# Weights that stay loaded on TensorE in a decode-attention kernel: one q slice for two score matmuls, 24 probability columns for four V matmuls, then a masked sum

## The chip, the cores and the metric

The kernel runs on one core of one Trainium2 chip. The metric is device time in microseconds (us), the median of several executions.

Engine names in the profile: PE is TensorE's matmuls, PEld its weight loads, DVE VectorE, ACT ScalarE, POOL GpSimd, SPq the queue from which the large transfers are issued.

## The reference, cut to what matters

```python
# B=2, Sq=1, Hq=16, Hkv=8, Sk=32768, Dh=256; all bf16
q = (x @ wq) as (B, Hq, 1, Dh);  k, v = caches (B, Hkv, Sk, Dh), each used by 2 q heads
scores = einsum("bhqd,bhkd->bhqk", q, k) * Dh**-0.5
o      = einsum("bhqk,bhkd->bhqd", softmax(scores), v)
a      = o.reshape(B, 1, Hq*Dh) @ wo
out    = g * a + (1 - g) * mlp(x)          # a small MLP, done while the first K arrive
```

The work is reading the two caches: 2 x 2 x 8 x 32768 x 256 bf16 values are 537 MB, and each is used for two heads only.

## The kernel before

There are 16 groups (batch x KV head). A group is two K tiles and two V tiles of 8.39 MB each. A ring of three slots in SBUF takes the tiles in the order K0 K1 K2 V0 K3 V1 K4 V2 ..., so that V runs two tiles behind K. A transfer into a slot is issued when TensorE has finished with the tile that was there.

```python
order: for i: K(i), then V(i - 2)         # slot = position in the order, modulo 3
released = {"K": S of that tile done, "V": PV of that tile done}
SP:  for d in order: wait(PE released the slot's last tile);  dma_start(slot, tile d)
```

DVE transposes each K tile in place in 8 blocks; after each block TensorE multiplies it with 8 slices of the query (each padded into a window, so that successive blocks fill different rows of one PSUM bank):

```python
def S(idx):                                # PE, K tile idx of group g, half t
    for blk in range(8):
        wait(DVE, T(idx, blk))
        for s in range(8):                 # 128x128 weights, 128x512 moving
            matmul(ps_s[g % 2], a_win(g, s, t * 8 + blk), kv[block blk, slice s],
                   start=first, stop=last)

def PV(v):                                 # PE, V tile; four column groups j at a time
    for kk in range(0, 8, 2):
        for r16 in range(16):
            matmul(ps_o[g % 2][32*j : 32*j + 4, 512], PT[:, r16, 4 columns], rows(kk, r16), ...)

def softmax(g):                            # DVE, after the second K tile's S
    MX  = reduce_max(ps_s[g % 2])          # 128x512
    ... maximum over partitions by two tiny matmuls (M1, M2); ACT: pexp = exp(ps_s - max)
    PT[g % 2] = transpose(pexp)            # 128x512
    ls2, L (matmul), rl = 1 / sum

def do_end(g):                             # DVE, after the group's second PV
    o_sb = copy(ps_o[g % 2])               # 128x512, one instruction
    ... OT: 4 tiny matmuls fold the column groups; attnT = OT * rl
# ... cut: projections, MLP, output product, the last group's V, helpers
```

## Time and profile before

| | before |
|---|---|
| time, median (range) | 1282.51 us (1282.38 to 1282.76) |
| PE busy / weight loads busy / DVE busy | 742.5 / 306.7 / 621.8 us |
| HBM read | 547.43 MB |
| instructions | 10758 |

No engine is busy for even 60% of the span, while the DMA engines are at 90% or more in every slice but the last. The line of queue 8 reads: 39 packets, 0.64 MB, 0.2% of the DMA engines' time; these are instructions being fetched for the engines.

Busy times in chosen stretches of before (us of each engine, with the number of instructions, then the granted TensorE clock, the DMA share and the rate):

```profile
core 0: us, PE busy (x) PEld busy (x) DVE busy (x) ACT busy (x) POOL busy (x), PEclk, DMA share, GB/s
104.00:136.00 32.00, 18.52 (x119) 7.18 (x112) 17.66 (x8) 0.00 (x0) 0.00 (x0) 0.79 1.00 433
...
117.80:1207.57 1089.77, 625.90 (x3780) 247.67 (x3780) 537.96 (x350) 22.29 (x94) 0.00 (x0) 0.77 1.00 433
```

In the 1090 us of the steady state the DMA share is 1.00. The rate, 433 GB/s, is that of the ceiling that the Trainium skill gives in "DMA: Bandwidth & Descriptors", section "Where 436 GB/s comes from" (435 GB/s).

The groups of the page of before that the change touches: line, engine, operation, output and inputs, shapes and count, then busy us and mean ns of one, then the idle time before them and what ended it.

```profile
L385 PE MATMUL ps_s<-ring,Abd 128*128 128x512 bf16 x2048 | 529.7, 415 | 435.4 <-DVE ring L604 434.8
L604 DVE STREAM_TRANSPOSE ring<-ring 128x2048 uint32<-128x2048 uint32 x256 | 565.2, 2276 | 418.3 <-DMA ring<-in_A_k_cache_dram 418.3
L385 PEld LDWEIGHTS ps_s<-ring,Abd 128*128 128x128 bf16 x2048 | 200.9, 103 | 758.2 <-DVE ring L604 347.3
...
L439 PEld LDWEIGHTS ps_o<-ring,PT 128*4 128x4 bf16 x1920 | 49.0, 97 | 82.0 <-issue 41.4
L638 DVE COPY o_sb<-ps_o 128x512 f32<-128x512 f32 x15 | 10.4, 692 | 80.7 <-PE ps_o L439 80.7
```

Read the waits from left to right: score matmuls wait 435 us for DVE's transposes, and these wait 418 us for K to arrive. Everything waits for DMA.

One group boundary in before, from the timeline (start us, duration us, what; SPq lines are transfers being issued):

```profile
409.88 0.33 SPq L311 DMA_DIRECT2D ring<-in_A_v_cache_dram  x1
413.45 0.33 SPq L311 DMA_DIRECT2D ring<-in_A_k_cache_dram  x1
428.93 17.66 DVE L604 STREAM_TRANSPOSE ring<-ring 128x2048 uint32<-128x2048 uint32 x8 [21.04 <-DMA ring<-in_A_k_cache_dram]
448.59 0.33 SPq L311 DMA_DIRECT2D ring<-in_A_v_cache_dram  x1
458.27 0.33 SPq L311 DMA_DIRECT2D ring<-in_A_k_cache_dram  x1
468.14 2.31 DVE L604 STREAM_TRANSPOSE ring<-ring 128x2048 uint32<-128x2048 uint32 x1 [7.75 <-DMA ring<-in_A_k_cache_dram]
```

K lands at 428.93; its scores are done 19.66 us later, which frees the slot for the V issued at 448.59. At that moment the K issued at 413.45 is still in flight; it lands at 468.14. So the DMA queue has 19.5 us of work when the slot is freed.

### The profile page before, as it was taken

What the parts mean: (1) busy time and instruction counts of PE and PEld (TensorE: products, weight loads), DVE (VectorE), ACT (ScalarE), POOL (GpSimd) and SP (SyncE); (2) the same over time, 40 slices, a digit from 0 to 9 for tenths busy, and PEclk for the clock granted to TensorE, in tenths of its full rate; (3) what the DMA queues carried; (4) which work ended last, traced back from release to release, by engine and by line L of the source; (5) the groups of instructions that cost most, each with busy time, mean ns of one, the idle gap of its engine ahead of it and who ended that gap; (6) DMA issues with size and microseconds to landing.
All of it is one profiled execution on the core that took longest, in us unless ns stands there. A gap on an engine that the chain in (4) does not pass through costs nothing.

```text
span 1281.1 us, 10758 instructions
## 1 busy us (share of the span) xinstructions
PE 742.5 (58%) x4977; PEld 306.7 (24%) x4977; DVE 621.8 (49%) x421; ACT 29.0 (2%) x118; POOL 3.5 (0%) x12
## 2 busy tenths in 40 slices
PE   4675557645476554665645666454765546656466
PEld 3222222212132121222212222121322212222134
DVE  1784446544365543456534465443655434565330
ACT  1000000000000000000000000000000000000000
POOL 1000000000000000000000000000000000000000
PEclk9887887776887777887777877777886778877786
DMA  9999999999999999999999999999999999999997
GB/s 409 428 435 436 432 432 430 435 432 438 426 433 438 434 424 432 443 429 430 432 440 428 426 438 438 430 424 438 434 432 432 432 432 434 435 432 428 436 401 293
DMA packets 12780, 548.12 MB, mean 428 GB/s; under 512 B 1336, under 2 KB 3520, under 8 KB 3904
## 3 DMA queue, kind: packets, MB, share of 16 engines
q1 hardware_dynamic: 12580, 547.43, 99.1%
q8 instruction: 39, 0.64, 0.2%
q10 hardware_dynamic: 156, 0.01, 0.0%
q14 instruction: 5, 0.04, 0.0%
HBM read 547.43 MB, written 0.00 MB: 427 GB/s over the span
## 4 chain that ended last, share of the span: by engine, by line
DMA 60%; DVE 26%; PE 11%; ACT 1%; SPq 1%; issue 0%; another core or an unknown queue 0%; ACTq 0%
DMA ring<-in_A_k_cache_dram 58%; DVE ring L604 23%; PE ps_o L439 7%; PE ps_s L385 2%; DMA ring<-in_A_v_cache_dram 2%; ACT pexp L536 1%; DVE PT L623 1%; DVE mx L609 1%; SPq L306 1%; PE ps_m L406 1%; PE ps_m L396 0%; PE ps_m L401 0%; DVE gmax L611 0%; DVE gmx L617 0%; ACT negm L532 0%
## 5 line engine op out<-in xcount | busy, mean ns | idle before, releaser
L385 PE MATMUL ps_s<-ring,Abd 128*128 128x512 bf16 x2048 | 529.7, 415 | 435.4 <-DVE ring L604 434.8
L604 DVE STREAM_TRANSPOSE ring<-ring 128x2048 uint32<-128x2048 uint32 x256 | 565.2, 2276 | 418.3 <-DMA ring<-in_A_k_cache_dram 418.3
L385 PEld LDWEIGHTS ps_s<-ring,Abd 128*128 128x128 bf16 x2048 | 200.9, 103 | 758.2 <-DVE ring L604 347.3
L439 PE MATMUL ps_o<-ring,PT 128*4 128x512 bf16 x1920 | 138.4, 453 | 1.0 <-DMA ring<-in_A_v_cache_dram 1.0
L439 PEld LDWEIGHTS ps_o<-ring,PT 128*4 128x4 bf16 x1920 | 49.0, 97 | 82.0 <-issue 41.4
L638 DVE COPY o_sb<-ps_o 128x512 f32<-128x512 f32 x15 | 10.4, 692 | 80.7 <-PE ps_o L439 80.7
L532 ACT ACTIVATE negm<-ps_m 128x1 f32<-128x1 f32 x16 | 2.7, 171 | 1175.4 <-PE ps_m L401 1175.4
L609 DVE TENSOR_REDUCE mx<-ps_s 128x1 f32<-128x512 f32 x16 | 11.1, 692 | 32.2 <-PE ps_s L385 32.2
L406 PE MATMUL ps_m<-ls,ones_f 128*128 128x2 f32 x32 | 7.8, 314 | 30.9 <-DVE ls L624 30.9
L415 PE MATMUL ps_m<-sel,o_sb 128*128 128x2 f32 x120 | 16.6, 260 | 12.0 <-DVE o_sb L638 12.0
L458 PE MATMUL ps_o<-PT,ring 128*128 128x2 bf16 x512 | 14.6, 165 | 14.5 <-DMA ring<-in_A_v_cache_dram 12.6
L623 DVE STREAM_TRANSPOSE PT<-pexp 128x512 bf16<-128x512 bf16 x16 | 11.4, 711 | 23.7 <-ACT pexp L536 23.7
L415 PEld LDWEIGHTS ps_m<-sel,o_sb 128*128 128x128 f32 x120 | 15.3, 196 | 19.6 <-DVE o_sb L638 19.6
L643 DVE TENSOR_TENSOR attnT<-ps_o,rl 128x2 bf16<-128x2 f32 x2 | 0.2, 158 | 37.6 <-PE ps_o L458 37.6
L458 PEld LDWEIGHTS ps_o<-PT,ring 128*128 128x128 bf16 x512 | 14.0, 103 | 15.5 <-DMA ring<-in_A_v_cache_dram 13.5
L406 PEld LDWEIGHTS ps_m<-ls,ones_f 128*128 128x128 f32 x32 | 6.5, 252 | 32.2 <-DVE ls L624 32.2
L396 PE MATMUL ps_m<-ident_f,mx 128*1 128x128 f32 x32 | 6.1, 270 | 12.5 <-DVE mx L609 12.5
L527 ACT COPY Abd<-qrep 32x16 bf16<-32x16 bf16 x64 | 12.7, 199 | 0.6
L643 DVE TENSOR_TENSOR attnT<-ps_m,rl 128x2 bf16<-128x2 f32 x30 | 3.4, 157 | 17.9 <-PE ps_m L415 17.9
L401 PE MATMUL ps_m<-ones_f,gmx 1*128 1x1 f32 x32 | 6.0, 256 | 9.9 <-DVE gmx L617 9.9
L536 ACT ACTIVATE pexp<-ps_s,negm 128x512 bf16<-128x512 f32 x16 | 11.0, 687 | 0.5
L468 PE MATMUL ps_f<-ring,attnT 128*2 128x448 bf16 x32 | 10.0, 488 | 0.7 <-DMA ring<-in_A_wo_dram 0.4
(58 smaller groups left out, 69.3 us busy)
## 6 DMA issues: line engine op xcount, KB each, us to landing
ring<-in_A_v_cache_dram SPq DMA_DIRECT2D x1, 4096.0 KB, 28.9
ring<-in_A_wo_dram SPq DMA_DIRECT2D x1, 3584.0 KB, 19.1
ring<-in_A_wq_dram SPq DMA_DIRECT2D x1, 3072.0 KB, 10.4
ring<-in_A_v_cache_dram SPq DMA_DIRECT2D x1, 2048.0 KB, 23.6
ring<-in_B_w_dram SPq DMA_DIRECT2D x1, 1568.0 KB, 18.0
ring<-in_B_w_dram SPq DMA_DIRECT2D x1, 1344.0 KB, 13.7
ring<-in_A_v_cache_dram SPq DMA_DIRECT2D x1, 1024.0 KB, 25.4
ring<-in_A_v_cache_dram SPq DMA_DIRECT2D x2, 512.0 KB, 26.4
```

The lines of the kernel that those rows point to most:

```text
L306: dma(lambda e, c0=c0, c1=c1: e.dma_start(ring[:, base + c0:base + c1], src[:, c0:c1]), f"pV{i}", ("piece", i))
L385: E.ins(lambda e, g=g, s=s, k=k, kv=kv, blk=blk, pss=pss: e.matmul(pss, a_win(g, s, k), kv[:, blk * CR:(blk + 1) * CR, s // 2, :, s % 2], ...
L406: E.ins(lambda e: e.matmul(ps_m[:, C_L:C_L + 2], ones_f[:, :], ls2[g % 2][:, :], start=True, stop=True), key=("L", g))
L415: E.ins(lambda e, j=j, half=half: e.matmul(ps_m[:, C_OT + 2 * j:C_OT + 2 * j + 2], o_sb[:, half * Dh + j:(half + 1) * Dh:2], sel[:, 2 * ha ...
L439: E.ins(lambda e, g=g, j=j, rows=rows, pt=pt, r16=r16, k=t * NCK + kk, n=n: e.matmul(ps_o[g % 2][32 * j:32 * j + 4, :].rearrange("p (k d) ...
L458: E.ins(lambda e, g=g, kv=kv, r=r, k=k, r16=r16, j=j, pt=pt, t=t: e.matmul(ps_o[g % 2][:, 2 * j:2 * j + 2], kv[:, r, j:Dh:2], pt[:, r16, k ...
L527: E.ins(lambda e, o=o, Q=Q: e.copy(o, qrep[32 * Q:32 * Q + 32, :, kvh, :, b]), key=(("A", g) if Q == 3 else None))
L536: E.ins(lambda e: e.activation(pexp[:, :], ps_s[g % 2][:, :], ACTF.Exp, bias=negm[g % 2][:, 0:1], scale=SCALE, accum_out=lsum[g % 2][:, 0: ...
L604: E.ins(lambda e: e.transpose(k_words(idx, blk), k_words(idx, blk)), key=("T", idx, blk))
L609: E.ins(lambda e: e.tensor_reduce(mx[i][:, :], ps_s[i][:, :], AX.X, ALU.max), key=("MX", g))
L623: E.ins(lambda e: e.transpose(PT[i][:, :], pexp[:, :]), key=("PT", g))
L638: E.ins(lambda e: e.tensor_copy(o_sb[:, :], ps_o[i][:, :]), key=("OS", g))
```

## The change

The intent is to load a set of weights into TensorE once and use it for several matmuls.

- Scores: one q slice serves two blocks of K, whose scores go to two PSUM banks; a stage waits for two transposes and then does 16 matmuls with 8 loads.
- V: 24 probability columns serve four matmuls into four banks. Of each 24 x 512 result only some entries are wanted, so the single copy of the output becomes eight multiply-by-mask-and-add steps.
- To make room in PSUM, the scores, the probabilities and the outputs are held once, no longer twice; softmax runs on 1024 columns, and the transpose of the probabilities now waits for the V product before it.

```diff
-        ps_s = [pm(f"ps_s{i}", [P, 512], dt.float32) for i in range(2)]
-        ps_o = [pm(f"ps_o{i}", [P, 512], dt.float32) for i in range(2)]
+        ps_s = pm("ps_s", [P, 1024], dt.float32)
+        ps_o = pm("ps_o", [P, 2048], dt.float32)
@@ a matmul without a weight load
+        def keep_matmul(e, o, w, x, start, stop, tile):
+            return e.add_instruction(mybir.InstMatmult(..., ldweights=False, ...))
@@ S
-                for blk in range(NCK):
-                    E.wait("dve", ("T", idx, blk))
+                for m in range(NCK // 2):
+                    E.wait("dve", ("T", idx, 2 * m + 1))
                     for s in range(NS):
-                        matmul(pss, a_win(g, s, k), block blk)
+                        for i in range(2):     # i == 0: matmul, i == 1: keep_matmul
+                            (ps_s bank i, a_win(s, w), block 2 * m + i)
@@ PV
+                    for r4 in range(0, CR, 4):
+                        for w in range(4):     # w == 0: matmul, else keep_matmul
+                            for j in range(4):
+                                (ps_o[32*j : 32*j + 24, bank w], PT[:, 24 columns], rows)
@@ do_end
-                    E.ins(lambda e: e.tensor_copy(o_sb[:, :], ps_o[i][:, :]), key=("OS", g))
+                    for c in range(8):         # c == 0: tensor_scalar, else scalar_tensor_tensor
+                        o_sb = ps_o[256 columns c] * mask[:, c] (+ o_sb)
@@ ... cut: single buffers, softmax order, query tile, set-up of the masks
```

## The prediction

> **What bounds the kernel now.** The DMA stream. The page reads 547 MB of HBM at 427 GB/s, with DMA at 9 tenths in all slices but the last. Busy times by stretch: between 117.8 and 1207.6 us it moved 433 GB/s at a DMA share of 1.00, with PE busy 57% and DVE 49%. The Trainium skill ("DMA: Bandwidth & Descriptors", "Where 436 GB/s comes from") puts the port ceiling at 435 GB/s, which this agrees with; its 358 GB/s per core is exceeded here. K lands every 39.2 us (428.93, 468.14), the time of two 8.39 MB tiles.
>
> The chain of waits seems to say otherwise: K transposes 23%, S and PV matmuls 9%, DMA of K 58%. But those K transfers take 47 to 49 us from issue although one tile needs 19.4: they queue behind another. The slack, from the order of issues: scores free a slot at 448.6, when the K issued at 413.5 is in flight until 468.1, so the V issued then could be 19 us later. PV frees a slot at 458.3; the V in flight lasts to about 487: 29 us.
>
> **What the change does.**
> - Scores: 2048 matmuls stay; half of the weight loads (98 ns each) go. Warm, eight matmuls take 1.9 us against 2.2 us for the transpose that feeds them: the loads were hidden, and TensorE already waited for DVE. PE now waits for two transposes and ends a tile with 16 matmuls: the slot is freed about 1.7 us later (19.6 to 21.3 us after K lands).
> - V: 1920 matmuls stay, loads fall to 480. Warm, 64 took 3.6 us; I expect 3.6 to 5.5.
> - Softmax on 1024 columns: maximum 0.69 to about 1.25 us, exponential 0.69 to about 1.2, transpose 0.71 to about 1.3 (scaled), but the transpose now stands behind the next V product. PV at a group's end starts 2 to 3 us later.
> - Output: one 0.69 us copy becomes eight masked operations of 128x256, estimated 0.43 us each from it: +2.9 us a group.
> - Buffers: scores, PT and ps_o become single. S of the next group waits for the exponential and the refilled query tile, ready 4 to 6 us after S ends, mostly well before the next K lands. Only at group 1, where K2 has landed at 79 us, does PE stall some 3 us, with a transfer still in flight.
> - Prologue: DVE starts 1.5 us later (bigger memset, masks), ahead of a wait for wq to 12.5 us.
>
> **On the critical path.** Every delay (2 to 5 us) is less than its slack (19 us or more), so DMA keeps its rate; no delay shows, and no saving. The tightest place is the tail: WO's issue moves from 1236.7 to about 1239, with V30 in flight until 1246.4; V30's product must wait for the masked sum of group 14, which I estimate ends near 1245. Up to 1.5 us may leak. The last V pieces and the 5.2 us after them stay.
>
> **Prediction: 1283.0 us**, 8 in 10 within 1279 to 1288. Faster by over 2%: 0.01; within 2%: 0.96; slower by over 2%: 0.03.
>
> **What would show it.** DMA share 1.00 and about 433 GB/s in the middle, K landings still 39 us apart; weight-load busy from 307 to about 165 us; DVE busy up about 60 us, its wait for K (418 us) down by less than 60; S end 21 us after K lands; K issue to landing about 2 us shorter.
>
> **What would make it wrong.** Kept-weight matmuls that serialise (V products 14 us instead of 3.6, pushing WO's issue past 1246, about 4 us in the tail only); a score stage over 38 us a tile; DMA slowed by extra DVE traffic. A gain would need DMA gaps that I do not see.

## More of the kernel before

The head of the page of before: busy time and share of the span for each engine with the number of its instructions, then the busy tenths of the DMA engines and the rate in 40 slices of the span, then the DMA queues.

```profile
span 1281.1 us, 10758 instructions
PE 742.5 (58%) x4977; PEld 306.7 (24%) x4977; DVE 621.8 (49%) x421; ACT 29.0 (2%) x118; POOL 3.5 (0%) x12
...
DMA  9999999999999999999999999999999999999997
...
q8 instruction: 39, 0.64, 0.2%
...
HBM read 547.43 MB, written 0.00 MB: 427 GB/s over the span
```

## The result

| | before | after |
|---|---|---|
| time, median (range) | 1282.51 us (1282.38 to 1282.76) | 1281.05 us (1280.70 to 1281.19) |
| instructions | 10758 | 8347 |
| weight loads, busy us | 306.7 | 176.3 |
| DVE busy us | 621.8 | 685.6 |
| K, issue to landing, median us | 49.0 | 46.2 |

The ratio of after to before is 0.9988, with a 95% interval of 0.9971 to 1.0005. A ratio is the mean time of one kernel's fast runs over that of the other's of the same rounds, so it is not quite the ratio of the medians. Yet the two ranges do not overlap: after is 1.45 us faster. The output is correct.

The head of the page of after:

```profile
span 1279.3 us, 8347 instructions
PE 733.6 (57%) x4917; PEld 176.3 (14%) x2453; DVE 685.6 (54%) x528; ACT 42.4 (3%) x182; POOL 2.5 (0%) x11
...
DMA  9999999999999999999999999999999999999997
...
q8 instruction: 29, 0.48, 0.2%
...
HBM read 547.43 MB, written 0.00 MB: 428 GB/s over the span
```

The same stretches as before, now of after:

```profile
104.00:136.00 32.00, 21.11 (x138) 4.05 (x53) 18.92 (x9) 0.00 (x0) 0.00 (x0) 0.84 1.00 431
...
117.80:1207.57 1089.77, 617.35 (x3724) 130.76 (x1484) 599.52 (x450) 34.83 (x154) 0.00 (x0) 0.77 1.00 433
```

The DMA share is 1.00 and the rate 433 GB/s, as before: the bound has not moved. Half the weight-load time is gone, and DVE has 62 us more to do in this stretch; neither shows in the rate.

The groups of the page of after:

```profile
L626 DVE STREAM_TRANSPOSE ring<-ring 128x2048 uint32<-128x2048 uint32 x256 | 565.1, 2275 | 318.4 <-DMA ring<-in_A_k_cache_dram 318.4
L399 PE MATMUL ps_s<-ring,Abd 128*128 128x512 bf16 x1024 | 426.1, 416 | 374.2 <-DVE ring L626 373.8
L272 PE MATMUL ps_s<-ring,Abd 128*128 128x512 bf16 x1024 | 422.7, 413 | 0.0
L399 PEld LDWEIGHTS ps_s<-ring,Abd 128*128 128x128 bf16 x1024 | 106.1, 104 | 785.1 <-issue 439.7
...
L458 PEld LDWEIGHTS ps_o<-ring,PT 128*24 128x24 bf16 x480 | 14.0, 107 | 100.3 <-issue 99.4
L665 DVE SCALAR_TENSOR_TENSOR o_sb<-ps_o,mask,o_sb 128x256 f32<-128x256 f32 x105 | 50.8, 484 | 3.7
```

The second score matmul of a pair (L272, no load) takes as long in the record as the first (413 and 416 ns). Better is the distance from start to start. With a load each, 36 matmuls in a row took 7.99 us in before, the last one's record 0.38: (7.99 - 0.38) / 35 = 217 ns. With every second load left out, 15 matmuls in after started from 407.06 to 410.09: 3.03 / 14 = 216 ns. The loads had been hidden entirely. The Trainium skill's "TensorE: Matmul & The Clock Gate", section "Back-to-back issue gap", has N / 2.4 + 2.5 ns = 216 ns for an isolated matmul of 512 columns and 131 ns sustained; both of these streams run at the former.

The same group boundary in after:

```profile
410.50 0.33 SPq L320 DMA_DIRECT2D ring<-in_A_v_cache_dram  x1
414.06 0.33 SPq L320 DMA_DIRECT2D ring<-in_A_k_cache_dram  x1
429.14 17.66 DVE L626 STREAM_TRANSPOSE ring<-ring 128x2048 uint32<-128x2048 uint32 x8 [22.37 <-DMA ring<-in_A_k_cache_dram]
450.58 0.33 SPq L320 DMA_DIRECT2D ring<-in_A_v_cache_dram  x1
...
461.35 0.33 SPq L320 DMA_DIRECT2D ring<-in_A_k_cache_dram  x1
461.36 1.25 DVE L646 STREAM_TRANSPOSE PT<-pexp 128x1024 bf16<-128x1024 bf16 x1 [5.53 <-PE ps_o L272]
...
463.00 3.60 DVE L665 SCALAR_TENSOR_TENSOR o_sb<-ps_o,mask,o_sb 128x256 f32<-128x256 f32 x7
...
467.86 2.31 DVE L626 STREAM_TRANSPOSE ring<-ring 128x2048 uint32<-128x2048 uint32 x1
```

Scores end 21.44 us after K lands (before: 19.66), the V slot is freed 3.1 us later, and DVE works at the output until 467.86, where the next K has just arrived. All of the engine work has become later, and K still arrives at 467.86, as it did at 468.14 in before: the delays vanish in the queue of transfers.

So two questions are left. Why is after 1.45 us faster, when the prediction found no saving on the path? And how much delay could the queue really have hidden?

### The profile page after: what moved, and what is told of

Its sections match the earlier page's. It is cut to its first block, busy times and chain, and to the rows that moved or that the text cites. A ratio compares the mean times of both kernels' runs of the same rounds, so it can differ in the third digit from the quotient of the medians.

```text
span 1279.3 us, 8347 instructions
## 1 busy us (share of the span) xinstructions
PE 733.6 (57%) x4917; PEld 176.3 (14%) x2453; DVE 685.6 (54%) x528; ACT 42.4 (3%) x182; POOL 2.5 (0%) x11
## 4 chain that ended last, share of the span: by engine, by line
DMA 58%; DVE 24%; PE 15%; ACT 2%; issue 1%; SPq 1%; another core or an unknown queue 0%; ACTq 0%
DMA ring<-in_A_k_cache_dram 56%; DVE ring L626 21%; PE ps_o L272 5%; PE ps_s L399 3%; PE ps_s L272 3%; DMA ring<-in_A_v_cache_dram 2%; PE ps_o L458 2%; DVE mx L630 1%; ACT pexp L555 1%; PE ps_m L422 1%; PE ps_m L417 0%; PE ps_m L412 0%; SPq L315 0%; DVE gmax L632 0%; DVE ls L641 0%
## 5 line engine op out<-in xcount | busy, mean ns | idle before, releaser
L399 PE MATMUL ps_s<-ring,Abd 128*128 128x512 bf16 x1024 | 426.1, 416 | 374.2 <-DVE ring L626 373.8
L272 PE MATMUL ps_s<-ring,Abd 128*128 128x512 bf16 x1024 | 422.7, 413 | 0.0
L399 PEld LDWEIGHTS ps_s<-ring,Abd 128*128 128x128 bf16 x1024 | 106.1, 104 | 785.1 <-issue 439.7
L272 PE MATMUL ps_o<-ring,PT 128*24 128x512 bf16 x1440 | 122.8, 456 | 0.0
L646 DVE STREAM_TRANSPOSE PT<-pexp 128x1024 bf16<-128x1024 bf16 x16 | 19.9, 1244 | 82.4 <-PE ps_o L272 82.4
L458 PE MATMUL ps_o<-ring,PT 128*24 128x512 bf16 x480 | 57.0, 465 | 0.0
L665 DVE SCALAR_TENSOR_TENSOR o_sb<-ps_o,mask,o_sb 128x256 f32<-128x256 f32 x105 | 50.8, 484 | 3.7
L630 DVE TENSOR_REDUCE mx<-ps_s 128x1 f32<-128x1024 f32 x16 | 19.6, 1225 | 59.8 <-PE ps_s L272 59.8
L458 PEld LDWEIGHTS ps_o<-ring,PT 128*24 128x24 bf16 x480 | 14.0, 107 | 100.3 <-issue 99.4
L641 DVE TENSOR_SCALAR ls<-par,lsum 128x2 f32<-128x2 f32 x16 | 3.7, 229 | 30.7 <-ACT pexp L555 30.7
L546 ACT COPY Abd<-qrep 32x16 bf16<-32x16 bf16 x128 | 19.4, 198 | 0.6
L555 ACT ACTIVATE pexp<-ps_s,negm 128x1024 bf16<-128x1024 f32 x16 | 17.8, 1115 | 0.5
L477 PEld LDWEIGHTS ps_o<-PT,ring 128*128 128x128 bf16 x512 | 14.1, 104 | 10.5 <-DMA ring<-in_A_v_cache_dram 8.5
```

What stands on the lines that cost most here:

```text
L272: return e.add_instruction(mybir.InstMatmult(name=f"I-{nc.next_id()}", engine=mybir.EngineType.PE, ldweights=False, ins=[e.lower_ap(x), e. ...
L399: fn = lambda e, o=o, x=x, st=st, sp=sp, s=s, w=w: e.matmul(o, a_win(s, w), x, start=st, stop=sp, skip_group_check=True)
L458: fn = lambda e, o=o, x=x, wt=wt, st=st, sp=sp, j=j: e.matmul(o, wt, x, start=st, stop=sp, skip_group_check=True)
L477: E.ins(lambda e, kv=kv, r=r, r16=r16, i=i, w=w, j=j, t=t: e.matmul(ps_o[:, 2 * j:2 * j + 2], kv[:, r, j:Dh:2], pt[:, r16, i, 2 * w:2 * w ...
L546: E.ins(lambda e, o=o, Q=Q, c=c: e.copy(o[:, :, c:c + 2], qrep[32 * Q:32 * Q + 32, :, kvh, :, b]), key=(("A", g) if (Q == 3 and c == 16) e ...
L555: E.ins(lambda e: e.activation(pexp[:, :].rearrange("p (r i a) -> p i r a", r=CR, i=2), ps_s[:, :].rearrange("p (i r a) -> p i r a", i=2, ...
```

## The experiments

Twelve kernels were run, each timed in the same rounds as the kernel before. Before measured 1282.51 to 1282.70 us.

### A theory for the 1.45 us: instruction fetch

The engines fetch their instructions by DMA. The Trainium skill, "Runtime: NRT & Kernel Launch", section "Instruction fetch mechanics", says that this happens in blocks of 16 KiB (256 instructions) over a DMA queue of its own, and that the cost of crossing a block is "mostly hidden". This trace agrees with the block: 39 packets and 0.64 MB are 16.4 KB each, and the 2411 instructions that the change saves make 10 packets fewer (29). If the fetched blocks take time from the same DMA engines that bring K and V, then they are not hidden in a kernel that is bound by those engines.

**Every weight load put back.** The changed kernel, but with loads for all matmuls.

```diff
         def keep_matmul(e, o, w, x, start, stop, tile):
-            return e.add_instruction(mybir.InstMatmult(..., ldweights=False, ...))
+            return e.matmul(o, w, x, start=start, stop=stop, skip_group_check=True)
```

> The changed kernel with every weight load put back (2464 more instructions: 1024 for scores, 1440 for V); all else of the change stays. The question is where the small measured gain of 1.45 us (1282.51 to 1281.05) comes from. Theory A (instruction fetch: the trace of before moves 0.68 MB of instructions on the same 16 DMA engines, that of after 0.54 MB): the 0.15 MB come back, so the time goes back to about 1282.5 us, and the instruction queue's bytes back to about 0.69 MB. Theory B (the gain comes from something else in the change, such as when transfers are issued): it stays at about 1281.0 us. Theory C (weight loads are really on the critical path, 100 ns each): it would rise by far more than 2 us. In all: weight-load busy time back to about 300 us, score stage as long as in after (21.4 us from K landing to its end).

Measured: 1282.88 us (1282.15 to 1283.61, 5 runs), ratio to before 1.0002 (0.9989 to 1.0014). The whole gain is gone. Weight loads are busy 315.4 us again, and the instruction queue is back at 38 packets. This agrees with theory A and rules out B. It does not yet tell fetching from loading: both came back.

**More instructions on an idle engine.** The kernel before, with 200 one-element copies on ACT in each of 15 groups.

```diff
                 chain(g)
+                for n in range(200):          # 15 groups; ACT waits for DVE and PE here anyway
+                    e.copy(junk[0:1, n:n + 1], ones_f[0:1, 0:1])
```

> The kernel before with 3000 tiny one-element copies on ScalarE, 200 in each of 15 groups, off every path (ScalarE sits idle 1175 us waiting for the next maximum). Theory A (instruction fetch shares the DMA engines with the data): 3000 instructions are 0.19 MB more to fetch, so by the ratio of the change (2411 fewer instructions, 1.45 us less) about 1.8 us slower than before, 1284.3 us. Theory B: no difference, 1282.5 us. If the copies take longer than the idle time of a group (over 0.36 us each) the run says nothing about either.

Measured: 1291.60 us (1291.22 to 1291.99), ratio 1.0070 (1.0057 to 1.0083). The direction is A's, but the size, 9.0 us, is five times what I expected. The copies took 188 ns each in the profile, started 93 ns apart, and ran in ACT's idle time.

The DMA queues on the page of this run:

```profile
q8 instruction: 39, 0.64, 0.2%
q14 instruction: 29, 0.24, 0.0%
```

ACT's instructions come over another queue than TensorE's, in blocks of some 8 KB: 29 packets where before has 5, while queue 8 has its 39 as ever. Why 24 small packets cost 9 us is seen when one looks at the parts of a transfer. The Trainium skill, "DMA: Bandwidth & Descriptors", section "Why a DMA increments its semaphore by 16 and not by 1", says that a transfer runs on up to 16 engines that finish independently, each adding one to the semaphore. In the traces each tile's semaphore indeed rises 16 times, and the times are recorded. Here are those of the last full tile (V30), in us from the start and in order of time (the trace does not say which engine is which):

```
V30, 16 increments   (packets of instruction queues 8 and 14)
fewer matmuls (20, 7)  1238.4 1238.5 1238.6 1238.8 1238.8 1238.9 1239.3 1241.1 1241.2 1241.3 1241.3 1241.4 1241.4 1241.8 1241.8 1242.2
after         (29, 7)  1238.3 1238.5 1238.6 1238.8 1238.8 1239.1 1239.4 1242.0 1242.8 1242.8 1242.9 1242.9 1243.0 1243.2 1243.4 1245.0
loads back    (38, 7)  1238.4 1238.4 1238.6 1238.7 1238.8 1239.1 1239.4 1242.1 1244.5 1244.5 1244.5 1244.5 1244.7 1245.1 1246.1 1246.1
before        (39, 5)  1238.1 1238.4 1238.7 1238.8 1238.9 1239.0 1239.1 1242.3 1244.2 1244.3 1244.5 1245.2 1245.3 1245.9 1246.0 1246.4
more PE       (70, 5)  1238.2 1238.3 1238.4 1238.5 1238.6 1238.7 1239.0 1242.1 1250.6 1250.7 1250.8 1250.8 1250.9 1251.2 1252.2 1252.6
more ACT      (39, 29) 1238.2 1238.2 1238.5 1238.6 1238.8 1239.0 1242.1 1244.3 1244.4 1244.4 1244.4 1244.6 1244.6 1246.0 1246.5 1255.6
```

The first six or seven parts land at 1238 to 1239 us whatever the kernel. The others are late. A tile is usable when the last part has landed, so the DMA engine that is furthest behind sets the time of the kernel. In the run with more ACT copies one single part is 9.1 us behind the fifteenth, which is just what the kernel lost. In before the last part is 8.3 us behind the first; early in the same trace (the seventh transfer into the ring, wq's two included) that was 2.0 us, and it grew all along, to 4.1 us at the 25th and 6.6 us at the 49th.

The lag of the last part behind the first also tells packets from copies. In the run with more ACT copies each of the 15 groups executes the same 200 copies in about 77 us, four transfers. But from the 17th transfer on the lag rises only where a packet of queue 14 lies between two landings, and else stays the same to within 0.15 us: 4.66 us for the 18th to 20th transfer, 5.33 to 5.35 us for the 21st to 24th, after one packet at 388.5 us; 6.72 us for the 27th, 8.03 us for the 30th, after two (540.5 and 553.3 us); 8.70 us for the 33rd, after one (624.1 us). That is 0.67 us for each 8 KB block on the engine that carries it, where the packet itself is recorded with 0.31 us. It also answers a rival, that something else which grows with the number of instructions, such as the profiler's own records, costs the time: that would be the same in every group.

**More instructions on TensorE.** The kernel before, with 124 one-by-one matmuls and their loads ahead of each score stage, where TensorE waits for K.

```diff
+                for n in range(124):
+                    e.matmul(ps_q[0:1, n:n + 1], ident_b[:, n:n + 1], ident_b[:, 0:1], start=True, stop=True)
                 for blk in range(NCK):
```

> The kernel before with 124 one-by-one matmuls (each with its weight load) ahead of every score stage, where TensorE waits for K: 7936 instructions more on TensorE, some 31 more fetch blocks of 16 KB. Instruction-fetch theory, with the size that the change itself shows (10 blocks fewer on this queue, 1.45 us less): about 4.5 us slower, 1287 us, and, if TensorE's blocks are spread over the 16 DMA engines as the even growth of the spread in before suggests, the last 4 or 5 of the 16 parts of each transfer move back together, not a single one as with ScalarE's queue (there the 15th part of V30 landed at 1246.5 us and the 16th at 1255.6). If all blocks of TensorE go to one engine: 31 x 0.38 = about 12 us. Rival (e2's loss came from ScalarE's own traffic): no change, 1282.6 us.

Measured: 1288.78 us (1288.64 to 1289.04), ratio 1.0048 (1.0036 to 1.0061): 6.1 us slower, between the two sizes that I gave. The line "more PE" above shows how: with 31 packets more (70), eight parts are late together, by about 6 us more than in before, and the first seven have not moved. So TensorE's blocks are spread, but over about half of the 16 engines and not over all, which is why I expected too little. Counted per late part, 31 / 8 = 3.9 more blocks made it 6.3 us later (1244.5 to 1250.8, the eleventh part): 1.6 us a block, while a fetch packet itself is recorded with 1.07 us.

The blocks go to these engines in turn. In this run the last part's lag rises by 1.5 us once in about eight packets of queue 8 and stays within 0.1 us in between: 9.82 us at the 40th transfer, 11.34 at the 48th, 12.85 at the 56th, 14.37 at the 63rd, with 40, 48, 57 and 64 packets fetched before. (The recorded times of the packets repeat after eight, too: in before 1069, 1061, 1099, 1099, 1086, 1018, 1018, 1074 ns, then 1066, 1061, 1100, 1107, 1085, 1018, 1018, 1074.) So one block is worth about 1.5 / 8 = 0.19 us on the kernel's time.

**Fewer instructions than after.** The changed kernel with two of the eight q slices left in the score product. Its output is wrong, which doesn't matter for the time.

```diff
-                    for s in range(NS):
+                    for s in (0, NS - 1):
```

> The changed kernel with only 2 of the 8 q slices of the score product (wrong result on purpose): 1536 matmuls and 768 weight loads fewer on TensorE, 9 fetch blocks of 16 KB fewer (29 to about 20); DMA data, DVE and the order of issues unchanged. Instruction-fetch theory, 0.2 us per block (31 blocks more cost 6.1 us): about 1.6 us faster than the changed kernel (1281.05), 1279.3 us, with the spread of the 16 parts of a late transfer down from 6.7 to about 5 us. Rival (the gain of the change came from elsewhere; TensorE's length is off the path): 1281.0 us.

Measured: 1279.44 us (1279.11 to 1279.61), ratio 0.9975 (0.9962 to 0.9989), 1.6 us faster than after, as the fetch theory had it (before measured 1282.58 and 1282.51); the spread of the parts of V30 is 3.8 us, less than I expected. The lines of queue 8 on the pages of this run, of the run with the loads back and of the run with more on TensorE:

```profile
q8 instruction: 20, 0.33, 0.1%
q8 instruction: 38, 0.62, 0.2%
q8 instruction: 70, 1.15, 0.4%
```

Put together, time against TensorE's fetch packets:

| kernel | packets | time, us | line through first and last |
|---|---|---|---|
| fewer matmuls | 20 | 1279.44 | 1279.44 |
| after | 29 | 1281.05 | 1281.12 |
| loads back | 38 | 1282.88 | 1282.80 |
| before | 39 | 1282.51 | 1282.99 |
| more PE | 70 | 1288.78 | 1288.78 |

The line rises (1288.78 - 1279.44) / 50 = 0.187 us a packet, which is also what the steps of the landings gave (0.19). It holds for kernels that differ widely in what TensorE does: adding useless matmuls, adding loads and leaving out score matmuls all fall on it to within 0.5 us. Ten packets fewer, and with them earlier parts that set the time, are the cause of the 1.45 us.

### How much delay does the queue hide?

The prediction rests on slack: the release of a slot may be some 19 us later. To test it, the last block of every K tile was transposed 2, 4 or 8 times more, which is an even number and leaves the data as they were. Each extra transpose takes 2.3 us on DVE.

```diff
+                if blk == NCK - 1:
+                    for n in range(4):        # 8 in the second run, 2 in the third
+                        e.transpose(k_words(idx, blk), k_words(idx, blk)); wait for it
                 e.transpose(k_words(idx, blk), k_words(idx, blk))   # T(idx, blk)
```

**Four more, about 9 us.**

> The kernel before with the last block of every K tile transposed 4 times more (an even number, so the result is unchanged): each score stage ends, and frees its slot, 4 x 2.2 = about 9 us later, and DVE is busy 280 us more. My theory (DMA is the bound, the slack of the release is 19 us): within 0.3% of before, about 1283 us, K still landing every 38.7 to 39.2 us, K's wait from issue to landing shorter by about 9 us. Rival (the chain of waits is literal: K transposes carry 23% of the time): every second K tile is in the chain, 16 x 9 = at least 140 us more, 11% slower.

Measured: 1315.02 us (1310.06 to 1315.68), ratio 1.0244 (1.0229 to 1.0260). Neither: 32 us slower. My slack was wrong as stated. Busy times in stretches of this run:

```profile
104.00:136.00 32.00, 20.39 (x100) 7.66 (x104) 31.86 (x15) 0.00 (x0) 0.00 (x0) 0.74 0.55 228
120.00:128.00 8.00, 0.77 (x4) 0.15 (x2) 7.90 (x4) 0.00 (x0) 0.00 (x0) 0.76 0.00 0
117.80:1207.57 1089.77, 667.47 (x3755) 255.14 (x3753) 789.69 (x460) 22.30 (x94) 0.00 (x0) 0.77 0.98 422
```

From 120 to 128 us the DMA moved nothing at all, with DVE busy throughout. At the start three K tiles come in a row (K0 K1 K2), so that DVE falls behind by three delays before the first V is used, and the queue runs dry. The first part of the 13th transfer landed at 252.1 us instead of 231.9: 20 us are lost there. After that some 12 us more are lost over the whole run.

**Eight more, about 18 us.**

> The same with 8 more transposes: about 18 us later per K tile. DVE then needs per group 2 x (17.7 + 17.7) + about 12 us of softmax and output = 83 us against the 77.4 us in which DMA brings a group. My theory: the slack is used up and DVE becomes the bound: about 16 x 5.4 = 87 us more, 1370 us, 6 to 8% slower, with DMA share clearly below 1. Rival (chain literal): 16 x 18 = 290 us or more, over 20% slower. If it stays within 1% of before, the slack is larger than I read.

Measured: 1492.04 us (1489.95 to 1492.48), ratio 1.1628 (1.1610 to 1.1646), with the queue of K and V at work in 85.9% of the span. DVE binds, as expected, but the size is neither mine (6 to 8%) nor the rival's (over 20%). A group takes 89.0 us (from the starts of the transposes of three groups at 299.52, 388.34 and 477.53 us) and not 83: between its transposes DVE works and waits 16.3 us where I had counted 12, and the transposes take 72.7 us where I had counted 70.8. Then 16 x (89.0 - 77.4) = 186 us of the 209, with the hole at the start besides.

**Four more, but only from the seventh K tile on.**

> As the run with 4 extra transposes (1315.0 us, 32.4 us over before), but only from the 7th K tile on, so that the three K tiles in a row at the start are left alone. Reading to be tested: of the 32 us some 19.5 were an empty DMA queue at the start (0 GB/s from 120 to 128 us), the rest a rate of 428 instead of 433 GB/s later on. Then this run loses 8 to 13 us: 1291 to 1296 us, with no slice near 255 GB/s. If the start alone was to blame: within 2 us of before. If the delay itself costs per tile all along: near 1310 us.

Measured: 1293.75 us (1291.79 to 1294.20), ratio 1.0084 (1.0070 to 1.0098), 11 us over before, and after the first slice (405) none ahead of the tail is below 413 GB/s (in the first run one had 255). So the two losses of the first run are apart: about 20 us at the start and 11 us after it. The latter is slack too: in this run the first part of V30 landed at 1249.4 us instead of 1238.1 and the last at 1251.9, a spread of 2.6 us instead of 8.3. The parts that are usually ahead had to wait for their slot to be issued. The 19.5 us of work that I read off the queue was that of the engine furthest behind; the foremost engines are up to 8 us ahead of it and run dry first. (This is how I read the landings; no run singles out an engine.) But V30's last part is only 5.6 us late. The other half of the loss lies in the tail: WO (the weights of the output product), the next large transfer after V30, was issued at 1253.44 us, 1.5 us after even V30's last part had landed, where before issued it at 1236.74 us, 9.6 us ahead of that landing; the last part of the whole V cache then landed at 1286.34 us instead of 1275.82, 10.5 us late.

**Two more, about 4.5 us: the size of the largest delay in the change.**

> The kernel before with 2 extra transposes of the last block on every K tile: its slot is freed about 4.5 us later, the size of the largest delay in the change (2 to 5 us). Slack theory: hidden entirely, within 2 us of before (1282.6 us). Rival (release delays always leak in part, in proportion: 32.4 us for 9 us of delay): about +16 us, 1299 us.

Measured: 1288.46 us (1287.47 to 1289.70), ratio 1.0044 (1.0031 to 1.0058): 5.8 us slower, where I expected nothing and the rival 16. The stretch at the start, and the steady state, of this run:

```profile
104.00:136.00 32.00, 25.58 (x154) 9.72 (x152) 29.50 (x14) 0.00 (x0) 0.00 (x0) 0.89 0.88 373
...
117.80:1207.57 1089.77, 681.45 (x3847) 260.44 (x3845) 667.01 (x406) 22.30 (x94) 0.00 (x0) 0.78 1.00 432
```

There is a hole at the start. V1 was issued at 118.95 us, when the transfer ahead of it (K3) had landed at 117.65. The first part of the 13th transfer is 5.15 us late, and the first part of V30 at the end of the run is still 5.1 us late (1243.2 instead of 1238.1). In the steady state 4.5 us of delay are hidden fully. A second hole is in the tail: V30's last part is 3.4 us late (1249.8 us), but the last part of the V cache 5.9 us (1281.75 instead of 1275.82). WO was issued at 1247.57 us, 4.3 us after V30's first part had landed; in before it was issued 1.4 us ahead of that.

**The same two transposes in the changed kernel.**

> The changed kernel with the same two extra transposes per K tile that cost the kernel before 5.8 us, all of it at the start, where V1 was issued at 119.0 us, after the transfer ahead of it had landed at 117.7. In the changed kernel V1 was issued at 109.2 us, 5.6 us later than in before (103.6); 15.4 us more makes 124.5 us, so the hole at the start should be about 5.6 us wider: about 11 us over the changed kernel, 1292 us, and none of it in the steady state. If the slack is a steady-state matter: within 2 us of 1281. If the release delay of the change had eaten no slack: 1286.9 us.

Measured: 1296.31 us (1293.73 to 1300.77), ratio 1.0107 (1.0090 to 1.0124), 15.3 us over after, and with an unusual scatter. V1 was issued at 124.03 us, and the hole at the start is 10.4 us by the first part of the 13th transfer (242.3 against 231.95 in after), 5.2 us wider than in the kernel before; this part came as expected. But the median lost about 5 us more than that, so some leaks later as well (432 GB/s from 600 to 1200 us where after has 433 to 434), where the changed kernel's own delays (1.8 and 3.1 us) add to the 4.5. What makes it scatter I did not find out.

How much room is left in the changed kernel at these two places? At the start V1 is issued at 103.60 us in before, and the parts of the transfer ahead of it land from 115.76 to 117.77; in after V1 is issued at 109.16 us, 5.6 us later, and the parts land from 115.84 to 117.98: 6.7 us to spare by the first part, 8.8 us by the last. In the tail the transfer is WO:

```profile
1236.74 0.38 SPq L301 DMA_DIRECT2D ring<-in_A_wo_dram  x1
1236.20 0.38 SPq L310 DMA_DIRECT2D ring<-in_A_wo_dram  x1
```

The first line is of before, the second of after. V30's parts land from 1238.10 to 1246.36 us in before and from 1238.34 to 1245.01 in after: 2.1 us to spare by the first part, 8.8 us by the last. The foremost engines have the least room in the tail; at the start the delays of three K tiles add up (15.4 us for V1 in the run with two more transposes).

### What would the change be worth if DMA did not bind?

Three kernels with the K and V transfers cut to a quarter of the tile (the first three K tiles and the last V tile are whole; the rest of a slot keeps stale data). Their outputs are wrong, which doesn't matter for the times.

```diff
-                    e.dma_start(cut(slot_of[d], 0, SLOT), src)
+                    n = SLOT if kind == "K" and idx < 3 else SLOT // 4
+                    e.dma_start(cut(slot_of[d], 0, n), src[:, 0:n])
```

The kernel before, cut:

> The kernel before with K and V transfers cut to a quarter of each tile (the rest of a slot keeps stale, finite data; wrong result on purpose), so that DMA no longer binds and the engines' own time shows. From the chain in before: per group 35.4 us of K transposes plus about 12.5 us from the end of the last transpose to the end of the output step: 48 us, x 16 plus start and tail of about 70: 840 us, within 60.

Measured: 864.18 us (863.60 to 864.36), within the range.

The changed kernel, cut:

> The changed kernel with the same cut. In after, from the end of the last transpose of a group (446.8 us) to the end of the output step (467.9) pass 21.1 us, against 13.8 in before: so 55 us per group, 7 us more x 16: about 110 us slower than the cut kernel before (some 13%). If keeping the weights were worth something once DMA is out of the way, it would be faster instead.

Measured: 960.91 us (960.25 to 961.69), 11% slower than the cut kernel before (96.7 us, 6.0 a group). The changed kernel, cut, with all loads put back:

> The changed kernel with the same cut and every weight load put back. If loads hide behind the matmuls (eight score matmuls took 1.9 us warm either way, 64 V matmuls 3.6 us), the same as the cut changed kernel within 1%. If kept weights save TensorE time: slower by up to 30 us.

Measured: 962.70 us (961.83 to 963.87). Keeping the weights is worth 0.2%, even here. The first group of each of the first two, the transposes, shows who binds without DMA (before cut, then after cut):

```profile
L605 DVE STREAM_TRANSPOSE ring<-ring 128x2048 uint32<-128x2048 uint32 x256 | 563.3, 2272 | 6.3 <-DMA ring<-in_A_k_cache_dram 6.3
```

```profile
L627 DVE STREAM_TRANSPOSE ring<-ring 128x2048 uint32<-128x2048 uint32 x256 | 563.3, 2274 | 7.3 <-DMA ring<-in_A_k_cache_dram 7.3
```

DVE hardly waits for K any more (418 us in the full kernel). It is DVE's work, with the waits on PE inside a group's softmax and output, that makes the time, and the change lengthens just these: a maximum over 1024 columns, the transpose behind the V product, eight masked steps.

## Why the prediction was right

The prediction was 1283.0 us within 1279 to 1288; the measured time is 1281.05.

- *DMA binds, and keeps its rate:* right. Share 1.00 and 433 GB/s in both.
- *Loads were hidden; TensorE waits for DVE:* right. 217 ns and 216 ns from start to start, and 0.2% between the cut kernels with and without the loads.
- *Sizes:* the slot is freed 21.4 us after K lands (predicted 21.3); weight loads busy 176 us (165); DVE 64 us busier (60); maximum 1.23 us (1.25), exponential 1.12 (1.2), transpose 1.24 (1.3); masked steps 0.48 us (0.43); 64 V matmuls still about 3.6 us warm; K from issue to landing 2.8 us shorter (2).
- *"Its wait for K (418 us) down by less than 60":* wrong. It fell by 100 us, to 318. I had only counted DVE's added work (64 us) and not that it also waits longer inside a group, for the scores (59.8 instead of 32.2 us) among others.
- *"The tightest place is the tail":* not refuted, but the leak of up to 1.5 us did not come. From the landing of the last K, WO's issue came 2.3 us later than in before, as I estimated; but that K landed 2.8 us earlier (1204.70 instead of 1207.55 us), so on the clock WO was issued 0.5 us earlier. The output step of group 14 ended at 1242.8 us with V30's last part landing at 1245.0. To the start, where three K tiles follow each other, the prediction gave only a stall of some 3 us; V1's issue moved by 5.6 us there. In the run with two more transposes both places ran dry, the start for all parts and the tail for the foremost.
- *"No delay shows, and no saving":* the first half is right for this change; the second is the step that failed, by 1.45 us. The term left out was the instruction fetch, whose blocks run on the same DMA engines: 10 blocks fewer, 0.15 to 0.19 us each. It does not matter at 2%, but it is the whole measured difference.
- *Slack of 19 us or more:* right in kind and too large. In the steady state 4.5 us vanish, but over the whole run they cost 5.8 us, at the start and in the tail; 9 us cost 11 us even with the start spared. The change, with 2 to 5 us, stayed inside. That part owes something to luck: the margin that held lay between the 4.5 us that vanished and the 9 us that did not, and was not the 19 us predicted.

## What to carry to other kernels

Before removing work from an engine, find out what that engine waits for: here 1024 plus 1440 weight loads could go without a trace, because they ran behind matmuls that themselves waited for transposes that waited for DMA. In a kernel that is bound by DMA, the time is that of the DMA engine furthest behind, so look at how far apart the parts of one transfer land, and count what else those engines carry; instructions are among it. A slack read from the steady state should be checked again at the start and in the tail, where the order of transfers is another one, and against the foremost DMA engines, which run dry first.

## What the Trainium skill lacked or had wrong

- "Runtime: NRT & Kernel Launch", section "Instruction fetch mechanics", calls the cost of crossing a fetch block mostly hidden. It does not say that the blocks delay data transfers; in this DMA-bound kernel they do: 0.19 us per block of TensorE on the kernel's time (20 to 70 blocks, 1279.4 to 1288.8 us), and 9.0 us for 24 blocks more on ACT. It has 16 KiB as the size of a block; ACT's were 8 KB here (24 packets of 8192 bytes for 3000 copies), TensorE's 16 KB.
- No page that I found says onto which DMA engines the blocks go. With 31 blocks more for TensorE eight of a transfer's 16 parts landed late together (by 6 us), in steps of 1.5 us for each eighth block; with 24 blocks more for ACT a single one did (by 9 us).
- "DMA: Bandwidth & Descriptors", section "Where 436 GB/s comes from", says that for transfers from HBM the limit of about 358 GB/s per core binds (below its table, where one core alone has 425 GB/s, the same page limits the 358 to both cores of a pair streaming; the sentence itself does not). This single core read 433 GB/s from HBM for 1090 us.
- "TensorE: Matmul & The Clock Gate", section "Back-to-back issue gap", gives about 131 ns as the sustained spacing of matmuls of 512 columns with their loads. Here it is 217 ns, the isolated figure of the same section.
